# The last head group's output sums dealt anew over its slots, and weight maxima kept in columns, in a two-layer attention and spectral-filter kernel

## The chip, the core and the metric

One core of one Trainium2 chip. TensorE (PE) multiplies matrices and writes its sums to PSUM; VectorE (DVE), ScalarE (ACT) and GpSimd (POOL) work on elements; SyncE (SP) issues nearly all transfers. Each engine runs its own queue of instructions in order, and the engines wait for each other through semaphores. The metric is the device time of one launch in microseconds, median of the runs. All times in the text are microseconds (us) unless marked ns; times inside the profiled execution count from its first instruction.

## What is computed

Two attention blocks and two spectral filters in turn, each on a layer norm of its input and added to it, with S = 2048 rows, D = 1024 columns and 32 heads of 32:

```python
x = x + _A_ref(_layernorm(x), A_wqkv, A_wo)
x = x + _B_ref(_layernorm(x), B_w_r, B_w_i)
x = x + _A_ref(_layernorm(x), A_wqkv, A_wo)
x = x + _B_ref(_layernorm(x), B_w_r, B_w_i)
```

`_A_ref` projects to q, k and v, takes `softmax(q k^T / sqrt(32)) v` for each head and multiplies by `wo`. `_B_ref` is a real 2-D FFT over rows and columns, a product with complex weights `w_r + i w_i`, and the inverse FFT.

## The kernel before

One attention and one filter make a layer; the program runs two layers. Products of float32 data are made of float16 halves: a value is scaled and split into a high and a low part (`split`), and each product is three matmuls (high by high, high by low, low by high).

**Attention.** The heads go in 8 groups of 4 (`NG`). A group has 4 chunks of 512 query rows (`NCH`) by 16 tiles of 128 key rows (`NKT`), so 64 units. `S` (line 552) makes one unit's scores: 12 matmuls into two tiles of the pool `psS`, which has three tiles of two PSUM banks; the exponentials (line 562) read them on ScalarE into the pool `at_p` of eight buffers. `PV` (line 568) multiplies them by V, for two units at a time on every even unit; `add` (lines 579 and 581) keeps the running sums of the softmax on VectorE; `fin` (from line 583) turns these into factors at the end of a chunk, and `out` rounds the chunk's result to two halves. In the last group that result, `olast[c]`, stays in SBUF; it is made at the sixth unit of the following chunk.

Two units make a slot, 32 in a group. Behind an odd unit's scores the loop places other matmuls, which it draws from generators (`filler`, `wo_parts`): the projections of later groups, and in the last two groups the output product with `wo`. That product has 12 row tiles of 128 rows that are done here (the last four are done in the tail), each of 1024 columns in two halves. A half has 8 x 3 matmuls of 512 columns; those of the first seven head groups (21) can be made early. `wo_part` (line 456) makes these 21 into the one bank of the pool `psX`, and VectorE evacuates them with the residual added (line 466). `wo_rest` (line 496) makes the six that are left for a tile, three for each half, into a tile of `psS`; `wo_last` (line 470) evacuates it (line 475), takes the statistics of the next layer norm (line 477) and stores the rows (line 478); `mvs` holds the statistics of the 12 tiles. Four halves of 21 are placed in group 6. In group 7 each slot has either one half or one rest: the first rest stands in slot 11, and from there on a rest alternates with a half until all 20 halves and 12 rests are placed. In a slot with a rest, the six matmuls directly follow the odd unit's scores.

The order on PE and ACT in this part is the program's (`manual_schedule`). The order on VectorE, GpSimd and SyncE is made when the program is built, by a planner that takes the earliest ready instruction by its own estimate of times.

**The attention tail** (from line 679). The last four row tiles' output sums, the last chunk's `fin` and `out`, and the layer norm and first fold of all 16 row tiles for the filter, on VectorE for the larger part.

**The filter.** Its first loop (33 turns of `t1` and `fa`, lines 787 to 816) transposes on PE, multiplies, and splits the result on ACT (line 804) and VectorE (line 805). Its second loop goes over 32 units (`fb`, `fc`, `binv`, `cinv`): `loadw` (line 827) loads a unit's weights, GpSimd turns signs in them (line 846), and `fc` multiplies them in (lines 901 to 906: VectorE and GpSimd). A third loop transforms back.

**The flags.** While layer 0 runs, the kernel takes the largest magnitude of `wqkv` (lines 260 and 261, 48 pieces), `wo` (lines 784 and 785, 16 pieces, loaded for this in line 780 by `absmax`) and the filter weights (lines 837 and 838, 32 pieces): a reduction of a piece to one column, then a maximum with a running column. `combine_flags` (line 1124) decides from them at the end whether a general version must run instead; with these inputs it does not.

Of the kernel before, what the change touches and what calls it, by code (L numbers as in the profile page):

```python
# [226 lines left out]
class Weights:  # L227
# [5 lines left out]
    def prep(self, ph):  # L233
# [10 lines left out]
        st = []  # L244
# [11 lines left out]
        for i, (h, l, _) in enumerate(sl):  # L256
            split(nc, h, l, st[i], SW)
            if self.flag is not None:
                wm = ap.sm.tile([128, 1], F32, name="wm")
# [10 lines left out]
def attention(nc, tc, layer, ap, xin, yd, wts, wo, cst, dram, flags):  # L270
# [212 lines left out]
    def wo_parts():  # L483
        load_o(0)
        load_o(1)
        for t in [2, 3, 0, 1] + list(range(4, 12)):
# [7 lines left out]
    mvs = sm.tile([128, 24], F32, name="mvs")  # L494

# [112 lines left out]
    fill, lwo, wof = filler(), load_wo(), wo_parts()  # L608
    left, parts, rests = 16, 20, list(range(12))

# [14 lines left out]
    with tc.manual_schedule(engines={mybir.EngineType.PE, mybir.EngineType.Activation}):  # L625
        for g in range(NG):
# [3 lines left out]
            for u in range(NCH * NKT):  # L630
# [43 lines left out]
        run(wof)  # L674
        for t in rests:
            wo_rest(t)
    with tc.manual_schedule(engines={mybir.EngineType.PE}):
# [72 lines left out]
def spectral(nc, tc, ap, yd, xout, a, cst, fast, flags=None, nxt=None):  # L750
# [25 lines left out]
    def absmax(i):  # L776
# [5 lines left out]
        while len(wos) == 3 or (wos and i == 15):  # L782
            m = p3.tile([128, 1], F32, name="wom")
            nc.vector.tensor_reduce(m, wos.pop(0), axis=AX.X, op=ALU.max, apply_absolute_value=True)
            nc.vector.tensor_max(flags["w"], flags["w"], m)

# [40 lines left out]
    def loadw(i):  # L827
# [7 lines left out]
        if flags is not None:  # L835
            m = p2.tile([128, 1], F32, name="wbm")
            nc.vector.tensor_reduce(m, wt, axis=AX.X, op=ALU.max, apply_absolute_value=True)
            nc.vector.tensor_max(flags["wb"], flags["wb"], m)
        sa = fs.index(0) if g == 0 and 0 in fs else None
# [284 lines left out]
def combine_flags(nc, tc, pool, flags, cst):  # L1124

    f = pool.tile([128, 6], F32, name="f4")
    v = pool.tile([128, 1], F32, name="fv")
    nc.vector.tensor_reduce(v, flags["mv"][:, :, 1], axis=AX.X, op=ALU.min)
# [3 lines left out]
    nc.vector.tensor_scalar(f[:, 1:2], r, 1e20, None, op0=ALU.is_le)  # L1132
    nc.vector.tensor_scalar(f[:, 2:3], flags["w"], 1.0, None, op0=ALU.is_le)
    nc.vector.tensor_scalar(f[:, 3:4], flags["wb"], 2.0 ** -4, None, op0=ALU.is_le)
    nc.vector.tensor_scalar(f[:, 0:4], f[:, 0:4], -1.0, 1.0, op0=ALU.mult, op1=ALU.add)
    nc.vector.tensor_scalar(f[:, 4:5], flags["w"], 2.0 ** -7, None, op0=ALU.is_ge)
    nc.vector.tensor_scalar(f[:, 5:6], flags["wb"], 2.0 ** -12, None, op0=ALU.is_ge)
    with tc.tile_pool(name="flag_ps", bufs=1, space=PSUM) as ps:
# [18 lines left out]
def build(nc, tc, a):  # L1157
    with ExitStack() as ctx:
# [9 lines left out]
        for h in range(4):  # L1168
# [4 lines left out]
            "mv": cp.tile([128, 32, 2], F32, name="fmv"),  # L1173
            "w": cp.tile([128, 1], F32, name="fw"),
            "wb": cp.tile([128, 1], F32, name="fwb"),
# [3 lines left out]
        nc.vector.memset(flags["w"], 0.0)  # L1179
        nc.vector.memset(flags["wb"], 0.0)  # L1180
        nc.vector.memset(flags["r"], 0.0)
# [4 lines left out]
        for t in range(2):  # L1186
            nc.sync.dma_start(ap.x[:, t], x[t * 128:(t + 1) * 128, :])
        wts = [Weights(nc, ap, a["wp"], None if layer else flags["w"]) for layer in range(2)]
        for layer in range(2):
# [47 lines left out]
```

## Time and profile before

| What | us |
|---|---|
| Runs (three) | 3885.0, 3885.8, 3886.59; median 3885.8 |
| The profiled execution's own time | 3887.92 |
| Span from its first to its last instruction | 3886.0 |
| Granted TensorE clock, mean | 0.988 |
| Busy: TensorE, VectorE, ScalarE, GpSimd | 3738.1, 3181.9, 2901.1, 304.1 |
| Last head group, layer 0 (first scores to the tail's first matmul) | 1414.30 to 1647.25 |
| Attention tail, layer 0 | 1647.25 to 1705.26 |
| Filter, first loop and second loop, layer 0 | 1705.26 to 1755.1, to 1918.4 |
| Last head group and tail, layer 1 | 3340.5 to 3573.45, to 3621.3 |

A row of the profile names an engine, a line of the kernel, an operation, what it writes and reads (`out<-in`), and how often; a number in square brackets is the time for which the engine stood idle ahead of it, and what ended that wait. PEld is TensorE's loading of stationary operands, which overlaps its matmuls. A matmul's printed duration overlaps the next one's, so the pace is read from starts.

### The profile page before, as it was taken

How to read it: one execution, taken by the hardware profiler on the slowest of the kernel's cores; microseconds unless marked ns; L12 is line 12 of the kernel's file. 1: busy time of each engine (PE TensorE's matmuls, PEld its weight loads, DVE VectorE, ACT ScalarE, POOL GpSimd, SP SyncE). 2: the span in 40 equal slices, each digit the busy share in tenths (PEclk: the TensorE clock that was granted, in tenths of full speed). 3: DMA queues.
4: the chain of work that ended last, by engine and by line, in shares of the span. 5: the costliest groups of instructions: out<-in, count | busy, mean ns of one | idle time of the engine just before them, and what ended most of it. 6: DMA issues, size and time to landing. Idle time of an engine off the chain costs nothing.

```text
span 3886.0 us, 79635 instructions
## 1 busy us (share of the span) xinstructions
PE 3738.1 (96%) x32951; PEld 1644.2 (42%) x32951; DVE 3181.9 (82%) x3967; ACT 2901.1 (75%) x3567; POOL 304.1 (8%) x386
## 2 busy tenths in 40 slices
PE   6999999999999999989989999999999999999998
PEld 4322433343234233368854334333433432333788
DVE  6689899989998987966675998989899889788544
ACT  4578887888788865657855888888888888666686
POOL 1000000000000000014320000000000000000143
PEclk9999999999999999999999999999999999999999
DMA  8000000000000221134270000000000002111333
GB/s 204 15 12 23 12 12 17 18 12 18 12 26 7 73 70 64 62 142 140 62 179 12 15 23 12 12 18 18 12 20 12 23 12 90 53 69 66 147 99 105
DMA packets 165575, 194.08 MB, mean 50 GB/s; under 512 B 74961, under 2 KB 120657, under 8 KB 164177
## 3 DMA queue, kind: packets, MB, share of 16 engines
q1 hardware_dynamic: 164912, 188.82, 15.6%
q8 instruction: 260, 4.26, 0.5%
q14 instruction: 115, 0.93, 0.1%
q10 hardware_dynamic: 288, 0.07, 0.0%
HBM read 123.83 MB, written 48.23 MB: 44 GB/s over the span
## 4 chain that ended last, share of the span: by engine, by line
PE 73%; DVE 12%; issue 7%; ACT 3%; DMA 3%; POOL 1%; SPq 0%; DVEq 0%; ACTq 0%; POOLq 0%
PE o L568 20%; PE s L558 17%; PE x L340 12%; PE x L384 7%; PE x L443 6%; DVE R L581 3%; ACT p L562 2%; PE ps L862 2%; PE ps L800 2%; PE s L587 1%; PE ps L791 1%; DMA w<-in_w 1%; PE s L443 1%; PE o L384 1%; PE ps L977 1%
## 5 line engine op out<-in xcount | busy, mean ns | idle before, releaser
L562 ACT ACTIVATE p<-s,bias 128x1024 f32<-128x1024 f32 x2048 | 2169.7, 1112 | 575.4 <-PE s L558 564.5
L581 DVE TENSOR_TENSOR R<-R,p 128x1024 f32<-128x1024 f32 x1792 | 2089.0, 1218 | 139.4 <-ACT p L562 136.3
L568 PE MATMUL o<-p,R 128*32 128x512 f32 x8192 | 985.5, 599 | 0.0
L340 PE MATMUL x<-big,wqk 128*128 128x512 f16 x2880 | 684.2, 383 | 17.0 <-DVE Q L168 6.3
L558 PEld LDWEIGHTS <-R 32*128 32x128 f16 x12288 | 233.0, 92 | 769.3 <-issue 654.3
L340 PEld LDWEIGHTS <-wqk 128*128 128x128 f16 x3072 | 277.3, 98 | 452.9 <-issue 159.1
L558 PE MATMUL s<-Q,R 32*128 32x512 f16 x6144 | 433.0, 378 | 12.0 <-ACT p L562 10.7
L558 PE MATMUL s<-R 32*128 32x512 f16 x6144 | 432.3, 379 | 8.2 <-ACT p L562 6.7
L568 PEld LDWEIGHTS o<-p,R 128*32 128x32 f32 x8192 | 213.8, 109 | 524.6 <-issue 524.0
L384 PEld LDWEIGHTS <-big 128*128 128x128 f16 x3072 | 296.5, 100 | 155.5 <-issue 73.9
L384 PE MATMUL x<-wv,big 128*128 128x256 f16 x2688 | 324.1, 277 | 34.5 <-DMA big<-hl 34.5
L579 DVE SCALAR_TENSOR_TENSOR R<-p 128x1024 f32<-128x1024 f32 x128 | 153.9, 1203 | 196.1 <-ACT p L562 195.7
L443 PE MATMUL x<-big 128*128 128x512 f16 x1050 | 237.4, 380 | 0.0
L365 POOL PARTITION_ALL_REDUCE mall<-mqk x16 | 40.7, 2542 | 2333.8 <-DVE mqk L359 2322.5
L443 PEld LDWEIGHTS <-big 128*128 128x128 f16 x1344 | 126.2, 98 | 178.0 <-issue 34.6
L910 DVE TENSOR_TENSOR H<-G,H 128x512 f16<-128x512 f32 (+1 forms) x68 | 46.5, 683 | 105.4 <-ACT H L909 105.3
L862 PE MATMUL ps<-cbi,H 128*128 128x256 f16 (+1 forms) x792 | 99.2, 273 | 6.0 <-ACT H L909 3.7
L855 ACT COPY U<-ps 64x256 f32<-64x256 f32 (+1 forms) x272 | 97.2, 357 | 8.4 <-PE ps L862 3.3
L855 ACT COPY B<-ps 64x256 f32<-64x256 f32 (+1 forms) x272 | 97.1, 357 | 6.7 <-PE ps L862 2.4
L862 PE MATMUL ps<-cb,big 128*128 128x256 f16 x780 | 96.3, 273 | 0.0
L805 DVE TENSOR_TENSOR big<-ps,big 128x512 f16<-128x512 f32 x64 | 44.5, 695 | 58.5 <-ACT big L804 58.5
L167 ACT ACTIVATE R<-x 128x512 f16<-128x512 f32 x88 | 52.7, 598 | 50.5 <-PE x L340 50.4
(429 smaller groups left out, 2992.5 us busy)
## 6 DMA issues: line engine op xcount, KB each, us to landing
wst<-in_wp SPq DMA_DIRECT2D x96, 256.0 KB, 3.0
R<-y SPq DMA_DIRECT2D x32, 512.0 KB, 5.4
w<-in_w SPq DMA_DIRECT2D x60, 256.0 KB, 2.7
od<-ohl SPq DMA_DIRECT2D x56, 256.0 KB, 2.4
big<-od SPq DMA_DIRECT2D x16, 896.0 KB, 6.7
y<-R SPq DMA_DIRECT2D x20, 512.0 KB, 2.7
R<-in_x SPq DMA_DIRECT2D x16, 512.0 KB, 5.8
wst<-in_wo SPq DMA_DIRECT2D x32, 256.0 KB, 3.0
```

The costliest lines, as they stand in the source:

```text
L167: nc.scalar.activation(hi, src, AF.Copy, scale=scale)
L340: nc.tensor.matmul(ps, a, b, start=d == 0 and i == 0, stop=d == 7 and i == 2)
L384: nc.tensor.matmul(ps[:, j], l, r, start=d == 0 and i == 0, stop=d == 7 and i == 2)
L443: nc.tensor.matmul(p, a, b, start=start and d == ds[0] and i == 0, stop=stop and d == ds[-1] and i == 2)
L558: nc.tensor.matmul(s[h // 2][:, h % 2], K[g][r, a, kt * 128:kt * 128 + 128], Q[g][r, b, c * 512:c * 512 + 512], start=i == 0, stop=i == 2)
L562: nc.scalar.activation(p, s[hf], AF.Exp, bias=bias[g], scale=SCALE / (SQ * SQ))
L568: nc.tensor.matmul(O[g, c][32 * h:32 * h + 32], V[g][:, kt, 32 * h:32 * h + 32], P[g, c, kt, h // 2][:, h % 2], start=kt == 0, stop=kt == ...
L579: nc.vector.scalar_tensor_tensor(acc[hf], P[g, c, 0, hf], 1e-34, p, op0=ALU.add, op1=ALU.add)
L581: nc.vector.tensor_add(acc[hf], acc[hf], p)
L800: nc.tensor.matmul(pa[:, j], tt[:, j], mm[:, g], start=True, stop=True)
L855: nc.scalar.copy(ov[64 * r:64 * r + 64, a0:a0 + m, x], tl[64 * x:64 * x + 64, :m, r])
L862: nc.tensor.matmul(out, l, r, start=k == 0, stop=k == len(mm_) - 1)
```

## The change

In the last group the 426 matmul steps of the halves are given out by a list, `share`, one number for each of the 32 slots, and the rests stand in slots 11, 12, 14, 15, 20, 22, 24, 26, 28, 29 and 30, in a slot behind its other matmuls. The first ten slots keep a whole half of 21 steps; slots 10 to 15 get 7 each, slots 16 to 27 get 11 and 10 in turn, and the last four get 12. Tile 11 has no rest: its halves are made of all 24 matmuls, and its statistics and store follow there.

Each maximum of a weight piece goes to a column of its own (64 columns for `wqkv` and `wo`, 32 for the filter weights), so the running maxima and the two memsets fall away, and `combine_flags` reduces the columns first. The reductions of `wo`'s pieces are tied to their place in the program: each comes on VectorE directly behind the split that was traced before it, in the filter's first loop.

```diff
-                nc.vector.tensor_reduce(wm, st[i], axis=AX.XY, op=ALU.max, apply_absolute_value=True)
-                nc.vector.tensor_max(self.flag, self.flag, wm)
+                nc.vector.tensor_reduce(self.flag.pop(), st[i], axis=AX.XY, op=ALU.max, apply_absolute_value=True)
...
-    def wo_part(c, t, dst):
+    def wo_part(c, t, dst, nd):
 
         x = xres(c, t)
+        st = sm.tile([128, 2, 6], F32, name="st")
         for n in range(2):
             p = bank()
-            m = wo_mm(p, c, t, n, range(7))
-            for _ in range(20):
+            m = wo_mm(p, c, t, n, range(nd))
+            for _ in range(3 * nd - 1):
                 next(m)
                 yield
             run(m)
             sl = slice(n * 512, n * 512 + 512)
             nc.vector.scalar_tensor_tensor(dst[:, sl], p, 1.0 / (SO * SW), x[:, sl], op0=ALU.mult, op1=ALU.add)
+            if nd == 8:
+                nc.vector.bn_stats(st[:, n], dst[:, sl])
+                if n:
+                    r0 = c * 512 + t * 128
+                    nc.sync.dma_start(yd[r0:r0 + 128, :], dst)
+                    nc.vector.bn_aggr(mvs[:, 8 * c + 2 * t:8 * c + 2 * t + 2], st)
             yield
...
-            yield from wo_part(t // 4, t % 4, wo_dst[t])
+            yield from wo_part(t // 4, t % 4, wo_dst[t], 8 if t == 11 else 7)
...
-    left, parts, rests = 16, 20, list(range(12))
+    left, rests = 16, {}
+    share = [21] * 10 + [7] * 6 + [11, 10] * 6 + [12] * 4
+    for t, n in zip(range(11), (11, 12, 14, 15, 20, 22, 24, 26, 28, 29, 30)):
+        rests[n] = t
...
-                    t = rests[0] if rests else 16
-                    if (t // 4 < c - 1 or t // 4 == c - 1 and kt >= 7) and (kt % 4 == 3 or not parts):
-                        wo_rest(rests.pop(0))
-                    elif parts:
-                        parts -= 1
-                        for _ in range(21):
-                            next(wof)
+                    for _ in range(share[u // 2]):
+                        next(wof)
+                    if u // 2 in rests:
+                        wo_rest(rests[u // 2])
...
-            m = p3.tile([128, 1], F32, name="wom")
-            nc.vector.tensor_reduce(m, wos.pop(0), axis=AX.X, op=ALU.max, apply_absolute_value=True)
-            nc.vector.tensor_max(flags["w"], flags["w"], m)
+            tc.keep_in_program_order(nc.vector.tensor_reduce(flags["wcol"].pop(), wos.pop(0), axis=AX.X, op=ALU.max, apply_absolute_value=True))
...
-            m = p2.tile([128, 1], F32, name="wbm")
-            nc.vector.tensor_reduce(m, wt, axis=AX.X, op=ALU.max, apply_absolute_value=True)
-            nc.vector.tensor_max(flags["wb"], flags["wb"], m)
+            nc.vector.tensor_reduce(flags["wb"][:, i:i + 1], wt, axis=AX.X, op=ALU.max, apply_absolute_value=True)
...
+    fw, fb = (pool.tile([128, 1], F32, name=n) for n in ("fwm", "fwbm"))
+    nc.vector.reduce_max(fw, flags["w"], axis=AX.X)
+    nc.vector.reduce_max(fb, flags["wb"], axis=AX.X)
```

More of the change, by code (lines that the diff above doesn't have):

```diff
@@ L453, in xres @@
         return x
-    def wo_part(c, t, dst):
+    mvs = sm.tile([128, 24], F32, name="mvs")
+    def wo_part(c, t, dst, nd):
         x = xres(c, t)
+        st = sm.tile([128, 2, 6], F32, name="st")
         for n in range(2):
             p = bank()
-            m = wo_mm(p, c, t, n, range(7))
-            for _ in range(20):
+            m = wo_mm(p, c, t, n, range(nd))
+            for _ in range(3 * nd - 1):
                 next(m)
@@ L485, in wo_parts @@
         load_o(1)
-        for t in [2, 3, 0, 1] + list(range(4, 12)):
+        for t in (2, 3, 0, 1, 4, 5, 6, 7, 8, 9, 10, 11):
             if t == 8:
@@ L489, in wo_parts @@
                 wo_dst[8], wo_dst[9] = two[:, 0], two[:, 1]
-            yield from wo_part(t // 4, t % 4, wo_dst[t])
+            yield from wo_part(t // 4, t % 4, wo_dst[t], 8 if t == 11 else 7)
             if t in (1, 7):
                 load_o(t // 4 + 2)
-    mvs = sm.tile([128, 24], F32, name="mvs")
     def wo_rest(t):
@@ L674, in attention @@
         run(wof)
-        for t in rests:
-            wo_rest(t)
     with tc.manual_schedule(engines={mybir.EngineType.PE}):
@@ L1124, in combine_flags @@
 def combine_flags(nc, tc, pool, flags, cst):
+    assert not flags["wcol"]
     f = pool.tile([128, 6], F32, name="f4")
+    fw, fb = (pool.tile([128, 1], F32, name=n) for n in ("fwm", "fwbm"))
+    nc.vector.reduce_max(fw, flags["w"], axis=AX.X)
+    nc.vector.reduce_max(fb, flags["wb"], axis=AX.X)
     v = pool.tile([128, 1], F32, name="fv")
@@ L1173, in build @@
             "mv": cp.tile([128, 32, 2], F32, name="fmv"),
-            "w": cp.tile([128, 1], F32, name="fw"),
-            "wb": cp.tile([128, 1], F32, name="fwb"),
+            "w": cp.tile([128, 64], F32, name="fw"),
+            "wb": cp.tile([128, 32], F32, name="fwb"),
             "r": cp.tile([128, 16], F32, name="fr"),
@@ L1178, in build @@
         }
-        nc.vector.memset(flags["w"], 0.0)
-        nc.vector.memset(flags["wb"], 0.0)
+        flags["wcol"] = [flags["w"][:, i:i + 1] for i in range(64)]
         nc.vector.memset(flags["r"], 0.0)
@@ L1187, in build @@
             nc.sync.dma_start(ap.x[:, t], x[t * 128:(t + 1) * 128, :])
-        wts = [Weights(nc, ap, a["wp"], None if layer else flags["w"]) for layer in range(2)]
+        wts = [Weights(nc, ap, a["wp"], None if layer else flags["wcol"]) for layer in range(2)]
         for layer in range(2):
```

9 lines of the change are left out of this document (4 added, 5 removed).

## The prediction, made before the changed kernel was run

> **What bounds the kernel now.** I read the page first, then the busy time by stage, then the single instructions of the stages that the change touches. The page says that TensorE (PE) does the work and that VectorE (DVE) is close behind.
>
> ```profile
> PE 3738.1 (96%) x32951; PEld 1644.2 (42%) x32951; DVE 3181.9 (82%) x3967; ACT 2901.1 (75%) x3567; POOL 304.1 (8%) x386
> ```
>
> An average over stages says nothing about one edit, so the next view is a table by stage: the last head group of layer 0 in two stretches (slots 0 to 9 and the start of slot 10; then slots 10 to 31), the attention tail of layer 0 and that of layer 1, the filter's first loop with two pieces of it, and the filter's second loop in layer 0 and in layer 1. Columns: stretch, length, busy time and count of PE, PEld, DVE, ACT, POOL; then PE clock, DMA share, GB/s.
>
> ```profile
> core 0 of [0], span 3886.0 us
> core 0: us, PE busy (x) PEld busy (x) DVE busy (x) ACT busy (x) POOL busy (x), PEclk, DMA share, GB/s
> 1414.30:1499.76 85.46, 85.46 (x667) 29.52 (x667) 57.62 (x62) 45.98 (x45) 0.00 (x0) 1.00 0.18 62
> 1499.76:1647.25 147.49, 142.15 (x1159) 45.77 (x1155) 132.27 (x148) 93.79 (x91) 0.00 (x0) 1.00 0.18 67
> 1647.25:1705.26 58.01, 42.88 (x205) 18.76 (x201) 49.28 (x105) 20.14 (x21) 11.62 (x33) 0.90 0.48 161
> 3573.45:3621.30 47.85, 42.72 (x205) 18.77 (x201) 39.43 (x74) 20.03 (x21) 11.64 (x33) 0.98 0.27 95
> 1705.26:1755.10 49.84, 49.84 (x384) 49.58 (x385) 21.18 (x33) 37.16 (x63) 0.00 (x0) 0.94 0.27 108
> 1715.00:1720.00 5.00, 5.00 (x43) 5.00 (x43) 2.58 (x4) 4.04 (x8) 0.00 (x0) 1.00 0.56 230
> 1720.00:1725.00 5.00, 5.00 (x42) 5.00 (x42) 2.26 (x4) 3.83 (x8) 0.00 (x0) 1.00 0.01 3
> 1755.10:1918.40 163.30, 153.08 (x1302) 135.92 (x1300) 104.46 (x256) 132.42 (x340) 70.49 (x102) 1.00 0.32 104
> 3670.60:3822.40 151.80, 147.60 (x1303) 134.27 (x1301) 73.97 (x190) 130.52 (x340) 70.65 (x102) 1.00 0.36 113
> ```
>
> Three things are to be seen. PE is never idle in the first stretch of the last head group, and is short of work by 5.3 us in the second. The two tails do the same matmuls (x205 each), yet layer 0's takes 10.16 us longer, with 9.85 us more on VectorE. The filter's first loop is PE from end to end, with VectorE busy for 21.18 of 49.84 us; its second loop is 11.5 us longer in layer 0 than in layer 1.
>
> **Part 1, the deal of the output sums.** One slot with a rest, PE's instructions in order:
>
> ```profile
> 1504.40 0.83 PE L558 MATMUL s<-Q,R 32*128 32x512 f16 x12
> 1505.16 1.92 PE L568 MATMUL o<-p,R 128*32 128x512 f32 x16
> 1507.01 0.82 PE L558 MATMUL s<-Q,R 32*128 32x512 f16 x12
> 1507.77 1.47 PE L443 MATMUL s<-big,ohl 128*128 128x512 f16 x6
> 1509.17 0.39 PE L558 MATMUL s<-Q,R 32*128 32x512 f16 x2
> 1510.05 0.82 PE L558 MATMUL s<-Q,R 32*128 32x512 f16 x10 [0.48 <-ACT p L562]
> 1510.80 1.92 PE L568 MATMUL o<-p,R 128*32 128x512 f32 x16
> 1512.65 0.40 PE L558 MATMUL s<-Q,R 32*128 32x512 f16 x4
> ```
>
> An unhindered block of scores takes 1505.16 - 1504.40 = 0.76 us. The block behind the rest takes from 1509.17 to 1510.80 = 1.63 us: after two matmuls it stands until ScalarE (ACT) has finished an exponential and freed a score buffer, because the rest itself has taken one of the three. The rest covers only 1509.17 - 1507.77 = 1.40 us of the two exponentials' wait. Each such slot loses 0.87 us. How many do, in this group:
>
> ```profile
> its engine sat idle before it (us, times) until:
>   ACT p L562: 5.3, 11
> ```
>
> Eleven (the twelfth rest has no scores behind it), so 11 x 0.87 = 9.6 us a layer. Layer 1 has the same structure, hence 19.1 us in all.
>
> After the change the rest always stands behind 7 to 12 other matmuls of the same slot, each 1.40/6 = 0.23 us, so 1.6 us or more is added to the 1.40, against 1.40 + 0.87 = 2.27 needed. The wait for the exponential is gone from all eleven. The matmuls themselves are the same: before 12 x (42 + 6) = 576 a layer, after 11 x 48 + 48 = 576. Slots 0 to 9 keep their 21 matmuls, so the first stretch stays as it is. The second becomes 147.49 - 9.6 = 137.9 us at best.
>
> What is late next is VectorE. It has the same work in that stretch, 132.27 us, so it goes from 90% to 96%. The wait to look at is the score buffer that a rest holds until its evacuation (L475) is done:
>
> ```profile
> 1509.02 1.23 DVE L581 TENSOR_TENSOR R<-R,p 128x1024 f32<-128x1024 f32 x1 [0.25 <-ACT p L562]
> 1510.16 1.22 DVE L475 SCALAR_TENSOR_TENSOR R<-s,R 128x1024 f32<-128x1024 f32 x1
> ```
>
> The rest ends at 1509.17; one running sum (L581) is ahead, and the evacuation ends at 1511.38. The scores that need that buffer stood at 1512.65, and without the lost 0.87 would stand at 1511.78: 0.40 us of slack. With a second running sum ahead (1510.16 - 1509.02 = 1.14 us) PE waits 0.74. The trace cannot show how often that happens in the new order, so I bound it: never (0), and at every one of the 22 rests (16.3 us). I take one rest in four, 22/4 x 0.74 = 4.1 us, since the scores at 1512.65 start without a wait for it, and VectorE has 4% left.
>
> Tile 11 is now summed whole (24 matmuls a half, through the other bank), with its two statistics and its aggregate on VectorE: the same instructions as its rest had, apart from two evacuations of 512 columns where there were two of 512 and one of 1024, about one running sum less. Its store and those of the other eleven stay at twelve, later or earlier in SyncE's queue by a slot or so; what reads them back comes only in the second loop. The residual loads go out one per tile as before. I cost these at nothing: the stretch's DMA share is 0.18, and the cover is the slack of a slot; without it a late residual load would hold one half's evacuation, at most 3 us once.
>
> **Part 2, wo's maxima.** Now the planner has put them into the attention tail of layer 0, where VectorE sets the pace:
>
> ```profile
> 1679.53 0.69 DVE L784 TENSOR_REDUCE wom<-wo 128x1 f32<-128x512 f32 x1 [1.78 <-DMA wo<-in_wo]
> 1680.13 1.22 DVE L475 SCALAR_TENSOR_TENSOR xres<-s,xres 128x1024 f32<-128x1024 f32 x1
> ```
>
> ```profile
> 1681.40 0.81 PE L443 MATMUL s<-big 128*128 128x512 f16 x3 [1.80 <-DVE xres L475]
> ```
>
> The reduction waits for its DMA, the evacuation stands behind it, and PE waits 1.80 us for the evacuation. Sixteen of 0.69 are 11.0 us of VectorE. Taken away, the tail should look like layer 1's, which is the same work without them: 58.01 - 47.85 = 10.2 us gained. Bounds: 0 (they are only moved, below) and 11.0 plus the sixteen running maxima.
>
> In the first loop the sixteen need 11.0 us of the 49.84 - 21.18 = 28.7 us that VectorE has free there, and the split (L805) behind each is late by 0.69 at most, with eight PSUM banks between it and PE. Their loads move too: three go out early as before, thirteen from inside the loop, each when a buffer is freed three reductions earlier, that is six turns of 49.84/33 = 1.5 us, 9 us ahead of use. On SyncE's queue they come behind the constants; the DMA engines are still at 0.56 in 1715 to 1720 and idle after. The first moved load goes out about seven turns after 1705.26, at 1716, and is wanted at turn 11, at 1722. So nothing is lost, with 0 to 5 us as bounds.
>
> A rule of the Trainium skill speaks against fixing them in place: "TensorE: Matmul & The Clock Gate", in the table that opens the page, gives VectorE a queue of 8 in strict first-in first-out order, so a reduction whose load is late holds everything behind it. The quoted pair (0.69 behind 1.78 of DMA wait, evacuation behind both) agrees. What it would do here is the third rival.
>
> **Part 3, maxima in own columns.** 96 running maxima and two memsets go; two short reductions come at the end and can be placed anywhere after the maxima. The 48 of wqkv and the two reductions lie beside a busy PE; I cost them at nothing, at 1 us if a few in the prologue are not covered. The 32 of the filter's weights, in the second loop:
>
> ```profile
> 1868.64 0.69 DVE L837 TENSOR_REDUCE wbm<-w 128x1 f32<-128x512 f32 x1
> 1869.24 0.41 DVE L902 TENSOR_TENSOR t__20499<-ps,w 128x256 f32<-128x256 f32 x1
> 1869.57 0.57 DVE L838 TENSOR_TENSOR fwb<-fwb,wbm 128x1 f32<-128x1 f32 x1
> ```
>
> ```profile
> 1869.40 0.73 POOL L846 TENSOR_TENSOR w<-w,sg 128x256 f32<-128x256 f32 x1 [2.59 <-DVE wbm L837]
> 1870.09 0.73 POOL L905 TENSOR_TENSOR G<-G,t__20499 128x256 f32<-128x256 f32 x1
> 1870.89 0.72 POOL L906 TENSOR_TENSOR G<-G,t__20499 128x256 f32<-128x256 f32 x1
> ```
>
> Here GpSimd's three run back to back, so the maximum (L838) is off the path: it delays products that GpSimd could not take sooner. It is on the path only where GpSimd waits:
>
> ```profile
> POOL G L905 <- DVE t__20435 L902: 0.5, 1, 0.5
> POOL G L905 <- DVE t__20160 L902: 0.5, 1, 0.5
> POOL G L905 <- DVE t__20306 L902: 0.5, 1, 0.5
> ```
>
> Three or four times 0.5: I take 2.0 us. The bounds are 0 and 11.5 us, layer 0's whole excess over layer 1; the reduction L837, which stays, carries most of that.
>
> The skill's page "SBUF — State Buffer", section "SBUF: two separate sides", says that a VectorE instruction with two SBUF inputs and a GpSimd instruction exclude each other for a whole instruction. The 0.57 us of a one-column maximum beside L846 agrees. By the rule alone each such maximum would give back its blocked time; by GpSimd's rows little of it reaches the path, and I keep 2.0.
>
> **The sum.** -19.1 + 4.1 - 10.2 - 2.0 = -27.2 us. The profiled execution took 3887.92 us (span 3886.0), which is 2.1 over the median of the three runs, 3885.8; taken off both, 3860.7 and 3858.6 us.
>
> **The rivals.** *VectorE becomes the bound of the last group:* every rest waits 0.74, 16.3 us, and the sum is -19.1 + 16.3 - 10.2 - 2.0 = -15.0, so 3871 us. For it: 96%; against: rests in before get their evacuation after one running sum.
> *Slower:* the planner puts four running sums ahead of each evacuation instead of one. The score buffer comes back 3 x 1.14 - 0.40 = 3.0 us late, 22 times, 66 us; with the other gains 3885.8 - 31.3 + 66 = 3921 us. It decides from 31.3/22 = 1.42 us of wait per rest, so about 1.6 running sums more than now. Against it: four are a slot's whole supply, and they would all have to be ready first.
> *wo's maxima are only moved:* each holds L805 and the loop grows by what the tail loses; -17.0, so 3869 us. For it: the fixed order; against: 28.7 us free.
> *The second loop falls to layer 1's pace* because the planner orders VectorE anew without the maxima: 9.5 us more, 3849 us. Against it: L837 stays.
>
> **Chances.** The forecast 0.69 (its own range 3850 to 3866), VectorE-bound 0.13, only moved 0.05, layer 1's pace 0.07, slower 0.06. The range 3847 to 3873 holds all but the slower case and the edges. A change under 0.2% (7.8 us) cannot be told from none here: faster 0.92, same 0.02, slower 0.06.
>
> **What would show it.** Waits of scores (L558) for ACT p in the last group near 0 instead of 11; the second stretch near 140 us; PE's wait for L475 small; layer 0's tail near 48 us with no L784 in it; the first loop at 50 us with sixteen L784 inside; the second loop near 161. Wrong would be: L558 waiting for DVE at most rests, or L805 late behind L784.

## The result, and the profile after

The changed kernel takes 3855.85 us (median of four runs, 3852.02 to 3858.89) against 3885.4 (four runs, 3882.65 to 3886.59): the ratio is 0.992, with a 95% interval of 0.9908 to 0.9932. The forecast was 3858.6, with a range of 3847 to 3873. The profiled execution took 3855.25 us, 32.7 less than that of before.

The page's line of busy times, changed kernel:

```profile
PE 3720.5 (97%) x32951; PEld 1640.1 (43%) x32951; DVE 3165.8 (82%) x3869; ACT 2898.3 (75%) x3567; POOL 303.0 (8%) x386
```

The matmuls are the same in number (x32951); VectorE has 98 instructions fewer. The same table by stage as before the change: the last head group of layer 0 in two stretches, the tails of layer 0 and layer 1, the filter's first loop, its second loop in layer 0 and in layer 1.

```profile
core 0 of [0], span 3853.3 us
core 0: us, PE busy (x) PEld busy (x) DVE busy (x) ACT busy (x) POOL busy (x), PEclk, DMA share, GB/s
1403.04:1488.50 85.46, 85.46 (x667) 29.52 (x666) 57.63 (x62) 45.92 (x45) 0.00 (x0) 1.00 0.19 62
1488.50:1629.44 140.94, 138.16 (x1159) 44.99 (x1155) 135.32 (x150) 93.50 (x91) 0.00 (x0) 1.00 0.20 74
1629.44:1677.28 47.84, 42.71 (x204) 18.79 (x200) 35.75 (x68) 19.99 (x21) 11.60 (x33) 0.98 0.32 110
3540.99:3588.84 47.85, 42.71 (x204) 18.78 (x200) 36.15 (x71) 19.99 (x21) 11.59 (x33) 0.98 0.25 86
1677.28:1726.81 49.53, 49.53 (x385) 49.26 (x385) 28.83 (x46) 37.08 (x63) 0.00 (x0) 0.95 0.48 175
1726.81:1889.73 162.92, 153.11 (x1302) 136.65 (x1300) 94.79 (x231) 131.99 (x340) 70.30 (x102) 0.98 0.34 106
3638.33:3789.59 151.26, 147.21 (x1303) 134.28 (x1300) 74.52 (x190) 130.25 (x340) 70.12 (x102) 1.00 0.35 113
```

Read against the table of before, stretch for stretch: the last group's first part is as it was (85.46), the second is 6.55 us shorter (147.49 to 140.94), layer 0's tail is 10.17 shorter and now equals layer 1's, the first loop has taken in thirteen of the sixteen reductions (VectorE 21.18 to 28.83) and is no longer than before, and the second loop is 0.4 shorter with 9.7 us less on VectorE.

**The last group.** Its waits on TensorE, in full (what waited, what for; us in total, times, longest):

```profile
PE s L563 <- DVE R L482: 2.8, 3, 1.4
```

The line numbers have moved by a few: L563 is the scores (L558 before), L482 the evacuation of a rest (L475). The eleven waits for an exponential are gone; three waits for an evacuation stand in their place. The longest of them, in the order of time, on TensorE and then on VectorE:

```profile
1522.47 1.92 PE L573 MATMUL o<-p,R 128*32 128x512 f32 x16
1525.83 0.83 PE L563 MATMUL s<-Q,R 32*128 32x512 f16 x12 [1.44 <-DVE R L482]
```

```profile
1519.47 3.44 DVE L586 TENSOR_TENSOR R<-R,p 128x1024 f32<-128x1024 f32 x3
1522.83 0.68 DVE L467 SCALAR_TENSOR_TENSOR R<-x,xres 128x512 f32<-128x512 f32 x1
1523.43 1.22 DVE L586 TENSOR_TENSOR R<-R,p 128x1024 f32<-128x1024 f32 x1
1524.56 1.22 DVE L482 SCALAR_TENSOR_TENSOR R<-s,R 128x1024 f32<-128x1024 f32 x1
```

The rest was done at about 1521.7. VectorE finishes a running sum, then takes the evacuation of a half (L467) and another running sum (L586), and only then the rest's; the score buffer comes back at 1525.78. Over both layers, none to two running sums come between a rest and its evacuation.

**The start of the second loop.** On VectorE, the first loop's last split, wo's last reduction and the second loop's first one; then TensorE's wait; then two of SyncE's own waits (L835 is the load of filter weights, L783 the load of a piece of wo):

```profile
1728.42 0.68 DVE L806 TENSOR_TENSOR big<-ps,big 128x512 f16<-128x512 f32 x1
1729.90 0.69 DVE L786 TENSOR_REDUCE fw<-wo 128x1 f32<-128x512 f32 x1 [0.80 <-DMA wo<-in_wo]
...
1734.47 0.69 DVE L837 TENSOR_REDUCE fwb<-w 128x1 f32<-128x512 f32 x1 [3.38 <-DMA w<-in_w]
```

```profile
1739.12 0.61 PE L861 MATMUL ps<-cbi,H 128*128 128x256 f16 x2 [4.22 <-ACT H L908]
```

```profile
SPq L783 <- DVE fw L786: 22.8, 9, 4.2
...
SPq L835 <- DVE fw L786: 3.7, 1, 3.7
```

The sixteenth reduction ends at 1730.59, after the last split, and the load of the first filter weights waits for it, because these weights take over the first loop's memory (its pools are closed there, and new ones opened). The two rows of before that answer to the last two:

```profile
1760.36 0.69 DVE L837 TENSOR_REDUCE wbm<-w 128x1 f32<-128x512 f32 x1 [3.74 <-DMA w<-in_w]
```

```profile
1765.09 0.39 PE L862 MATMUL ps<-cbi,H 128*128 128x256 f16 x2 [1.56 <-ACT H L909]
```

The first weights land 7.66 us after the second loop's first matmul (1734.47 less 1726.81), before the change 5.25 us (1760.36 less 1755.11). TensorE waits 4.22 us where it waited 1.56, and the two matmuls behind the wait take 0.61 instead of 0.39: the granted clock is 0.50 from 1737.10 to 1743.80. The first loop hides the reductions, but not the tail of the chain of loads.

**Where the time went, by stage.** Each length runs from the first matmul of a stage to that of the next; the last group is counted here to its last product with V.

| Stage | before | changed | difference | forecast |
|---|---|---|---|---|
| Groups 0 to 5, layer 0 | 1107.3 | 1097.7 | -9.6 | 0 |
| Last group, both layers | 2 x 232.42 | 2 x 225.87 | -13.1 | -15.0 |
| Tail, layer 0 | 58.54 | 48.38 | -10.2 | -10.2 |
| Second loop, layer 0 | 163.32 | 162.92 | -0.4 | -2.0 |
| Group 6, layer 1 | 182.47 | 184.99 | +2.5 | 0 |
| All the rest | | | -1.9 | 0 |

Two rows were not in the forecast, and the fourth was the sum of two larger things. The experiments are about these.

### The profile page after: what moved, and what is told of

Its sections match the earlier page's. It is cut to its first block, busy times and chain, and to the rows that moved or that the text cites. A ratio compares the mean times of both kernels' runs of the same rounds, so it can differ in the third digit from the quotient of the medians.

```text
span 3853.3 us, 79584 instructions
## 1 busy us (share of the span) xinstructions
PE 3720.5 (97%) x32951; PEld 1640.1 (43%) x32951; DVE 3165.8 (82%) x3869; ACT 2898.3 (75%) x3567; POOL 303.0 (8%) x386
## 4 chain that ended last, share of the span: by engine, by line
PE 73%; DVE 12%; issue 8%; ACT 3%; DMA 2%; POOL 2%; SPq 0%; DVEq 0%; POOLq 0%; ACTq 0%
PE o L573 19%; PE s L563 16%; PE x L338 12%; PE x L382 7%; PE x L441 6%; DVE R L586 4%; PE s L441 2%; PE ps L861 2%; PE ps L801 2%; ACT p L567 1%; PE s L592 1%; PE ps L792 1%; DMA wst<-in_wp 1%; PE ps L976 1%; PE ps L930 1%
## 5 line engine op out<-in xcount | busy, mean ns | idle before, releaser
L586 DVE TENSOR_TENSOR R<-R,p 128x1024 f32<-128x1024 f32 x1792 | 2085.4, 1219 | 111.2 <-ACT p L567 107.8
L563 PEld LDWEIGHTS <-R 32*128 32x128 f16 x12288 | 231.6, 92 | 760.3 <-issue 644.6
L563 PE MATMUL s<-R 32*128 32x512 f16 x6144 | 430.9, 378 | 10.6 <-ACT p L567 8.9
L563 PE MATMUL s<-Q,R 32*128 32x512 f16 x6144 | 425.4, 378 | 7.5 <-DVE R L482 5.5
```

What stands on the lines that cost most here:

```text
L563: nc.tensor.matmul(s[h // 2][:, h % 2], K[g][r, a, kt * 128:kt * 128 + 128], Q[g][r, b, c * 512:c * 512 + 512], start=i == 0, stop=i == 2)
L586: nc.vector.tensor_add(acc[hf], acc[hf], p)
```

## The experiments

The theory after this comparison: deal and tail do what the forecast says, the filter weights' columns gain about 5 us, and the chain of wo's loads takes as much away at the start of the second loop. Rivals: the second loop's gain is small, as forecast, and its start has another cause; and the gain in groups 0 to 5 is chance of the clock and not the change's.

Each ran beside the kernel before on the same chip; the ratios are to it. The deal and the maxima come first, then the parts of the maxima with what they led to; wqkv's stand near the end. They ran in three batches, and the median of the kernel before was another in each: 3885.55 us beside the deal alone, all the maxima, wo's alone and wqkv's alone; 3886.5 beside the filter weights' alone, wo's maxima earlier, the rests ahead and the rests spread; 3889.46 beside the others. Between batches the ratios are the better comparison.

**The deal alone.** The new shares, the rests' places and tile 11, with all maxima as before.

```diff
-    left, parts, rests = 16, 20, list(range(12))
+    left, rests = 16, {}
+    share = [21] * 10 + [7] * 6 + [11, 10] * 6 + [12] * 4
...
```

> Only the new deal of the output sums in the last group; all maxima as before. My theory: the eleven waits of the scores for an exponential go in both layers and a few waits for a rest's evacuation (3 a layer, 2.8 us in the changed kernel) come, so the last group is 6.6 us shorter in each layer, 225.9 instead of 232.4, and the run about 13 us shorter (3872). The attention tail of layer 0 stays at 58.5 and groups 0 to 5 of layer 0 stay as before, within what the granted clock does from run to run (each half-clock stretch costs about 1.5 us). Rival: the last group gains only because VectorE has no running maxima elsewhere or because of a new order that the whole change brings; then it stays near 232.

Measured: 3870.79 us, ratio 0.9956 (0.9943 to 0.997), 14.8 us less. The last group of layer 0 and its tail:

```profile
1413.60:1639.44 225.84, 223.08 (x1819) 74.43 (x1820) 192.36 (x211) 139.59 (x136) 0.00 (x0) 1.00 0.20 69
1639.45:1695.52 56.07, 43.24 (x209) 18.77 (x201) 46.76 (x102) 20.10 (x21) 11.93 (x33) 0.93 0.50 165
```

The group's gain is the deal's own, to 0.03 us. The tail is 2.5 us shorter though nothing in it was changed: VectorE's order in it is another, and the granted clock is 0.93 where it was 0.90. Which of the two does it is not shown.

**All the maxima, the old deal.**

```diff
-                nc.vector.tensor_max(self.flag, self.flag, wm)
...
-            nc.vector.tensor_max(flags["w"], flags["w"], m)
...
-            nc.vector.tensor_max(flags["wb"], flags["wb"], m)
...
```

> Only the maxima: own columns for all three weights and wo's reductions tied to the first loop; the deal as before. My theory: the tail of layer 0 falls from 58.5 to 48.4 us, both last groups stay at 232.4, the second loop loses 0.5 to 2. Groups 0 to 5 of layer 0 were 10.5 us shorter in the changed kernel: theory A, the 48 running maxima of wqkv were ahead of splits for which PE waits, and without them it falls below the length at which the clock is halved; then these groups are about 10 us shorter here too and the run is 21 us shorter, 3864. Theory B, the halved clock comes by chance of phase; then these groups are anywhere between 0 and 10 us shorter, and the run 11 to 21 us shorter.

Measured: 3869.37 us, ratio 0.9955 (0.9942 to 0.9969), 16.2 less. Tail 48.38, last groups 232.42 and 232.43, second loop 162.71, groups 0 to 5 of layer 0 1099.1. The halves of the change add up: 14.8 + 16.2 = 31.0 us against 29.5 for the whole.

**wo's maxima alone, tied.**

```diff
-            m = p3.tile([128, 1], F32, name="wom")
-            nc.vector.tensor_reduce(m, wos.pop(0), axis=AX.X, op=ALU.max, apply_absolute_value=True)
-            nc.vector.tensor_max(flags["w"], flags["w"], m)
+            tc.keep_in_program_order(nc.vector.tensor_reduce(flags["wcol"].pop(), wos.pop(0), axis=AX.X, op=ALU.max, apply_absolute_value=True))
...
```

> Only wo's maxima: columns of their own and tied to the first loop; wqkv, the filter's weights and the deal as before. My theory: the tail of layer 0 falls from 58.5 to 48.4 us, the first loop stays at 49.5 to 50 with sixteen reductions in it, nothing else changes by more than the clock's chance: 10 us less, 3875. Rival: the reductions hold the splits of the first loop, which grows by up to 10 us; then the run is unchanged.

Measured: 3882.75 us, ratio 0.9991 (0.9982 to 1.0001), 2.8 less, which is not clear of none. The tail and the second loop:

```profile
1649.04:1697.41 48.37, 43.24 (x208) 18.77 (x200) 39.55 (x72) 20.02 (x21) 11.64 (x33) 0.99 0.35 121
1747.41:1915.90 168.49, 155.35 (x1302) 137.21 (x1300) 106.53 (x263) 132.32 (x340) 70.52 (x102) 0.98 0.33 103
```

The tail gives its 10.2 us, and the first loop stays at 50.00, as the theory had it. But the second loop is 5.2 us longer than before, which neither theory had: half of the gain is lost a stage later. This pointed to the start of the second loop, and so to the next pair.

**The filter weights' maxima alone.**

```diff
-            m = p2.tile([128, 1], F32, name="wbm")
-            nc.vector.tensor_reduce(m, wt, axis=AX.X, op=ALU.max, apply_absolute_value=True)
-            nc.vector.tensor_max(flags["wb"], flags["wb"], m)
+            nc.vector.tensor_reduce(flags["wb"][:, i:i + 1], wt, axis=AX.X, op=ALU.max, apply_absolute_value=True)
...
```

> Only the filter weights' 32 running maxima go; wo's and wqkv's maxima and the deal as before. Theory A: the second loop of layer 0 falls from 163.3 to about 157.5 us, because the changed kernel's 162.9 is the sum of this gain, some 5.5, and of a loss at its start (the first weights of the second loop land 2.4 us later behind wo's last loads, and the clock is halved after a wait of 4.2 us); the run is 5 to 6 us shorter than before, 3880. Theory B (my prediction's sum): 2.0 us at most, the second loop near 161.5. Rival: nothing, 163, and the loop of 168.5 in the kernel with wo's maxima alone has another cause.

Measured: 3880.12 us, ratio 0.9985 (0.9976 to 0.9994).

```profile
1752.94:1913.95 161.01, 153.51 (x1303) 136.56 (x1300) 93.08 (x225) 132.29 (x340) 70.55 (x102) 0.99 0.33 105
```

The loop is 2.3 us shorter, which is theory B's number; the timed run is 6.4 us shorter (interval 2.3 to 9.3), which is theory A's. The trace decides: after a wait of 1.63 us at the loop's start this profile has a stretch at half clock (0.50 from 1763.90 to 1767.20), where the kernel before, after 1.56 us, has none. So the loop is cut in two. Its last two thirds, from the same product on, in the kernel before, in this one and in the changed kernel:

```profile
1811.00:1918.43 107.43, 100.64 (x845) 88.61 (x844) 68.24 (x163) 89.25 (x233) 46.36 (x68) 1.00 0.17 49
```

```profile
1811.00:1913.95 102.95, 98.90 (x845) 88.32 (x844) 59.48 (x143) 89.01 (x233) 46.20 (x68) 1.00 0.18 51
```

```profile
1787.10:1889.73 102.63, 98.84 (x845) 88.31 (x844) 59.27 (x144) 88.95 (x233) 46.23 (x68) 1.00 0.18 51
```

4.5 and 4.8 us less for the same 845 matmuls, while the first third is 2.2 us longer here than before (58.06 against 55.89). ScalarE's waits for GpSimd's last product in these last two thirds, before and changed:

```profile
ACT H L909 <- POOL G L906: 14.7, 20, 1.1
```

```profile
ACT H L908 <- POOL G L905: 10.0, 17, 1.1
```

4.7 us less, and 4.5 less with the filter weights' columns alone (10.2 in 17 waits). So the running maxima cost more than twice what I took. That they did it by delaying the chain from VectorE's products through GpSimd to ScalarE is what these waits suggest; the planner also orders VectorE anew without them, and no run parts the two.

**wo's maxima earlier.** The changed kernel, with the sixteen reductions in every turn from turn 10 to 23, done well ahead of the loop's end.

```diff
-        if i % 2:
-            absmax(i // 2)
+        absmax(i - 8)
```

> The changed kernel with wo's maxima in each turn of the first loop from turn 10 to 23 instead of in every second turn up to the end. Theory A (the last loads of wo hold up the second loop's first weights): the second loop of layer 0 starts with a PE wait of about 1.6 us instead of 4.2 and without a half-clock stretch, and is 157 to 158 us long instead of 162.9; the run 5 us shorter than the changed kernel, 3851. Rival: the reductions, now in each turn (0.68 of 1.48 us beside a split of 0.69), hold the splits and the first loop grows by 2 us or more. Rival: the start's wait has another cause; the second loop stays at 162.9.

Measured: 3853.76 us, ratio 0.9916 (0.9902 to 0.993). First and second loop, and TensorE's wait at the second loop's start:

```profile
1687.81:1737.49 49.68, 49.68 (x385) 49.41 (x386) 30.91 (x52) 37.13 (x63) 0.00 (x0) 0.95 0.50 180
1737.49:1895.88 158.39, 151.62 (x1302) 135.60 (x1300) 93.72 (x225) 132.34 (x340) 70.20 (x102) 1.00 0.34 107
```

```profile
1747.31 0.39 PE L860 MATMUL ps<-cbi,H 128*128 128x256 f16 x2 [1.41 <-ACT H L907]
```

Theory A holds: the wait is 1.41 us, the clock does not fall, and the second loop is 158.4, 4.5 us less, while the first loop is 0.15 longer. So in the changed kernel's 162.92, 4.5 us were the late weights and the clock behind them; without these the second loop would have gained 4.9. By the medians the whole run shows only 2.1 of the 4.5, within its scatter (3849.61 to 3862.44).

**wo's maxima not tied.** The changed kernel without the tie; own columns kept.

```diff
-            tc.keep_in_program_order(nc.vector.tensor_reduce(flags["wcol"].pop(), ...
+            nc.vector.tensor_reduce(flags["wcol"].pop(), ...
```

> The changed kernel without the tie of wo's maxima to their place in the program; own columns as in the changed kernel. Theory A: the tie alone takes them out of the attention tail; without it the planner puts them back there, the tail of layer 0 is 58 us and the second loop starts without its wait of 4.2 us and is 158 to 159 us long: 5 to 6 us longer than the changed kernel in sum, 3861. Rival: without the chain through the running maximum the planner leaves them out of the tail by itself, and the kernel is like the changed one, 3856, or better.

Measured: 3858.77 us, ratio 0.992 (0.9903 to 0.9936). Tail and second loop:

```profile
1635.29:1690.55 55.26, 43.24 (x208) 18.77 (x201) 45.65 (x87) 20.09 (x21) 11.55 (x33) 0.91 0.50 167
1739.65:1898.51 158.86, 151.58 (x1302) 135.58 (x1300) 93.14 (x225) 132.30 (x340) 70.73 (x102) 1.00 0.34 107
```

The planner puts all sixteen back into the tail, which is 6.9 us longer than the changed kernel's; the second loop is 4.1 shorter. The tie is what empties the tail, and it gives back more than half of that. The 2.8 us that are left do not show in the timed runs: the ratio is the changed kernel's, 0.992.

**The rests ahead of the other matmuls.** The changed kernel, same slots and shares, the two statements in the other order.

```diff
+                    if u // 2 in rests:
+                        wo_rest(rests[u // 2])
                     for _ in range(share[u // 2]):
                         next(wof)
-                    if u // 2 in rests:
-                        wo_rest(rests[u // 2])
```

> The changed kernel with each rest ahead of the other matmuls of its slot instead of behind them: the same shares and the same slots. My theory (the rest takes one of three score buffers, and what stands behind it must cover two exponentials): the 7 to 12 matmuls behind the rest cover the exponential as well as ahead of it, since both stand between the odd unit's scores and the next, so no wait for an exponential comes back; but the evacuation has 1.6 us or more longer, so the waits for it (three a layer, 2.8 us) shrink. The last group is then 223 to 226 us. Rival: the rest has to wait for its own buffer, which an exponential still holds, and loses 0.5 to 0.9 us in most of the eleven slots: the last group is 229 to 233.

Measured: 3856.22 us, ratio 0.9926 (0.9909 to 0.9943).

```profile
1405.30:1631.23 225.93, 223.97 (x1821) 74.41 (x1820) 192.10 (x211) 139.48 (x136) 0.00 (x0) 1.00 0.20 70
```

225.93 against 225.87: no difference, though the waits are others. The waits for an evacuation shrank from 2.8 us to 0.6, as the theory had it, and a rest waited once for its own buffer, for 0.2; but a wait of 1.1 us for a running sum came, and TensorE is busy for 0.9 us longer with the same matmuls (223.97 against 223.09), which stays unexplained. That the other matmuls stand in the same slot as the rest is what covers the exponential; on which side of it they stand does not matter.

**The rests spread, first try.** Rests in slots 11, 13, 15 and 17, the shares made even around them.

```diff
-    share = [21] * 10 + [7] * 6 + [11, 10] * 6 + [12] * 4
-    for t, n in zip(range(11), (11, 12, 14, 15, 20, 22, 24, 26, 28, 29, 30)):
+    share = [21] * 10 + [8, 7] + [9, 7] * 3 + [11, 10] * 5 + [12] * 4
+    for t, n in zip(range(11), (11, 13, 15, 17, 20, 22, 24, 26, 28, 29, 30)):
```

> The changed kernel with its rests in slots 11, 13, 15 and 17 instead of 11, 12, 14 and 15, and the 63 matmuls of slots 10 to 17 dealt as 8, 7, 9, 7, 9, 7, 9, 7. My theory (the three waits for a rest's evacuation, 0.93, 0.39 and 1.44 us, come where short slots with rests follow one another and VectorE is behind): they shrink to one or none, and the last group is 223 to 224.5 us in each layer instead of 225.9; the run is 3 to 5 us shorter. Rival: VectorE is behind by its whole work in these slots (the running sums of both units and the evacuation), wherever the rest stands; then the waits only move, and the group stays near 225.9.

Measured: 3862.72 us, ratio 0.9944 (0.993 to 0.9958): slower than the changed kernel, against the theory, though the two intervals just overlap (0.993 to 0.9932). The last group is 229.11 us. TensorE's waits in it:

```profile
PE x L441 <- DVE R L467: 4.0, 2, 2.6
PE s L563 <- DVE R L482: 0.2, 1, 0.2
```

The waits for a rest's evacuation did shrink, from 2.8 to 0.2. But two halves now end in the middle of a slot, and the next half, which needs the same single bank of `psX`, stands behind its evacuation (L467) with nothing between. The changed kernel's shares 7, 7, 7 and 11, 10 sum to 21: each half ends with its slot, and scores and products with V cover the evacuation. That property was in the list of numbers, and I had not seen it.

**Both, with the shares left alone.** Rests in slots 11, 13, 15 and 17, the changed kernel's shares, and the earlier maxima of wo.

```diff
-    for t, n in zip(range(11), (11, 12, 14, 15, 20, 22, 24, 26, 28, 29, 30)):
+    for t, n in zip(range(11), (11, 13, 15, 17, 20, 22, 24, 26, 28, 29, 30)):
...
-        if i % 2:
-            absmax(i // 2)
+        absmax(i - 8)
```

> The changed kernel with wo's maxima in each turn of the first loop from turn 10 to 23, and with its rests in slots 11, 13, 15 and 17 instead of 11, 12, 14 and 15, the shares left as they are, so that every half still ends with its slot. Theory A: e8_spread lost 3 us a layer because two halves ended in the middle of a slot and the next half had to wait for the one bank (4.0 us); with the shares left alone this wait is gone, and the waits for a rest's evacuation are fewer than the three of the changed kernel: the last group 223 to 225 us in each layer, the second loop of layer 0 158.4, the run 6 to 8 us under the changed kernel, 3848 to 3850. Rival: VectorE is behind in these slots by its whole work; the last group stays at 225.9 or above, and the run is 4 to 5 us under the changed kernel, 3851.

Measured: 3849.08 us (four runs, 3846.45 to 3852.84), ratio 0.9898 (0.9881 to 0.9915). The last group and the second loop of layer 0, and the waits in the group:

```profile
1406.23:1630.72 224.49, 223.02 (x1821) 74.39 (x1820) 191.91 (x211) 139.59 (x136) 0.00 (x0) 1.00 0.20 69
1728.77:1887.18 158.41, 151.46 (x1302) 135.59 (x1300) 92.89 (x225) 132.39 (x340) 70.65 (x102) 1.00 0.34 108
```

```profile
PE s L563 <- DVE R L482: 1.5, 2, 1.0
```

1.4 us less in each last group and 4.5 in the second loop make 7.3 us by stages; the median is 6.8 under the changed kernel's, and by the two ratios the difference is some 8.5. The two intervals against the kernel before overlap slightly (0.9908 to 0.9915).

**wqkv's maxima alone.** This and the two repeats that follow ask for the 9.6 us in groups 0 to 5.

```diff
-                nc.vector.tensor_reduce(wm, st[i], axis=AX.XY, op=ALU.max, apply_absolute_value=True)
-                nc.vector.tensor_max(self.flag, self.flag, wm)
+                nc.vector.tensor_reduce(self.flag.pop(), st[i], axis=AX.XY, op=ALU.max, apply_absolute_value=True)
...
```

> Only wqkv's 48 running maxima go, each piece's maximum has its own column; all else as before. Theory A (running maxima delay the splits that PE waits for): groups 0 to 5 of layer 0 are about 10 us shorter and no half-clock stretch is in them after 140 us, the run about 11 us shorter, 3874. Theory B (chance of phase): half-clock stretches in these groups are found here too, three or four of them, each 1.5 us; then the groups are 2 to 5 us shorter at most, from waits of 0.3 to 0.5 us less at each place.

Measured: 3882.17 us, ratio 0.9989 (0.998 to 0.9998), 3.4 less; groups 0 to 5 are 1102.6 us, 4.7 less than in the first profile of before. That is theory B's size, with two half-clock stretches after 140 us where A had none and B three or four. The four parts alone (14.8, 2.8, 6.4 and 3.4) add up to 27.4 us against 29.5 for the whole.

**The kernel before and the changed kernel, once more, unaltered.**

> The kernel before, once more. Theory B (which waits of PE are followed by a half clock is chance): groups 0 to 5 of layer 0 differ from the first profile's 1107.3 us by 2 us or more, with other places at half clock, while last groups, tails and groups 1 to 5 of layer 1 agree to 0.1 us. Rival: these groups repeat to 0.5 us, and the 10.5 us by which they were shorter in the changed kernel are the change's own.

> The changed kernel, once more. Theory B: groups 0 to 5 of layer 0 are 2 us or more longer than the first profile's 1097.7, with half-clock stretches in them, of which the first profile had none after 140 us; group 6 of layer 1 is not 185.0 again but anywhere from 182 to 185.5. Rival: both repeat to 0.5 us.

Groups 0 to 5 of layer 0 in one view each: before, before again, changed, changed again.

```profile
125.21:1232.52 1107.31, 1085.29 (x10201) 384.21 (x10201) 996.86 (x1078) 892.39 (x948) 23.53 (x24) 0.99 0.05 16
```

```profile
124.32:1236.96 1112.64, 1089.03 (x10201) 384.74 (x10201) 996.71 (x1078) 891.70 (x948) 22.36 (x24) 0.99 0.05 16
```

```profile
123.59:1221.26 1097.67, 1077.13 (x10201) 382.10 (x10202) 991.47 (x1041) 891.64 (x948) 26.21 (x24) 1.00 0.05 16
```

```profile
126.39:1227.03 1100.64, 1081.22 (x10201) 383.02 (x10201) 991.62 (x1041) 892.26 (x948) 26.25 (x24) 0.99 0.05 16
```

The same program differs by 5.3 and by 3.0 us here, while groups 1 to 5 of layer 1 agree to 0.3 us in all fourteen profiles. So theory B holds, and theory A in part: over all profiles of this study the five with running maxima of wqkv have 1106.0 to 1112.6 (mean 1108.8), and the nine without have 1097.7 to 1105.5 (mean 1100.8). By the traces' record of the granted clock, the five have 3 to 7 half-clock stretches in these groups after 140 us (mean 4.8), the nine have none to 4 (mean 2.0). So about 8 us in the mean goes with the change; the first pair's 9.6 held some luck. What remains open is why the timed gain of wqkv's columns alone (3.4, interval 0.8 to 7.8 us) lies at half of it; in that kernel's profile, group 6 of layer 1 takes 1.6 of its 4.7 us back (184.09 against 182.47).

Group 6 of layer 1 was 184.99 in the first profile of the changed kernel and 182.81 in the second, so the +2.5 does not come in every execution. Whether the change makes it likelier is open: it takes 184.0 us or more in five of the nine profiles without wqkv's running maxima, and 182.1 to 182.5 in all five with them. In the first profile of the changed kernel, ScalarE's split of a piece of wo came late, and the scores behind it:

```profile
3252.96 0.63 ACT L167 ACTIVATE big<-wst 128x512 f16<-128x512 f32 x1 [4.68 <-DMA wst<-in_wo]
```

## Why the prediction was right, and where it was right by luck

The forecast was 27.2 us, the medians differ by 29.5; the terms fit less well than their sum.

*The exponentials' wait* (-19.1): right. Eleven waits became none in both layers, and the deal alone gives the same group to 0.03 us. A group is 6.55 us shorter with 2.8 of new waits in it, so about 9.35 came back where 9.6 were forecast.

*The new wait for the evacuation* (+4.1, one rest in four at 0.74): right in kind and about in size. Three of eleven rests a layer wait, 2.8 us, so 5.6 in all. Each costs 0.93 on average and not 0.74, because the evacuation of a half can stand ahead too, which I had not counted. That VectorE would be at 96% in the second stretch was met, but from other figures: 135.32 of 140.94 us where I had 132.27 of 137.9. Some 3 us of its work came into the stretch from the tail (layer 1's tail: 39.43 before, 36.15 after, with the same matmuls). This did not make it the bound.

*wo's maxima out of the tail* (-10.2): met to 0.05 us. Layer 1's tail, the same work without them, was the right price tag.

*"So nothing is lost"* in the first loop: wrong, though the loop itself did not grow. I followed each load to its own reduction, found it 9 us ahead of use, and stopped there. Three of the sixteen reductions came behind the loop's last matmul. The last of the chain was not followed to what comes behind it on SyncE: the first weights of the second loop wait for the sixteenth reduction. 4.5 us, inside the 0 to 5 that I had named as the bound for it, but for another reason.

*The filter weights' running maxima* (-2.0): mis-sized; 4.8 to 4.9. I read three GpSimd waits of 0.5 us as all of the path. The wait that shrank with the loop was ScalarE's, for GpSimd's last product, 14.7 us in twenty waits, and I had left it out. A one-column maximum took 0.15 us at the shortest and 0.57 in the median of the loop's 32, like the one beside GpSimd's product in the prediction's rows. VectorE had 20 of them in the last two thirds of the loop, where its busy time fell by 8.97 us (68.24 to 59.27), of which 4.8 reached the end. The Trainium skill ("SBUF — State Buffer", section "SBUF: two separate sides") says that a VectorE instruction with two SBUF inputs and a GpSimd instruction that reads SBUF shut each other out for the whole instruction; the 0.57 against 0.15 agrees, and I gave the rule too little.

These last two errors nearly cancel, and that is luck: 4.9 gained and 4.5 lost make -0.4, against -2.0.

*wqkv's maxima at nothing, "1 us if a few in the prologue are not covered"*: wrong. They do not lie beside a busy TensorE everywhere: it waits for single splits on VectorE in each group, and each such wait can cost a stretch at half clock besides. About 8 us by the means of the profiles, 3.4 by the timed run. This gain was not in the sum. Without it the change would be worth 21.5 to 26.1 us, less than the forecast; that the total came so near is luck in part.

The rivals: VectorE as the bound did not come; three rests of eleven waited, not all. The slower case is refuted: none to two running sums came ahead of an evacuation, not four. The reductions did not hold the splits of the first loop (49.53 us).

## What to carry to other kernels

Where loads are moved to the end of a stage, follow the last of them to the first load of the next stage: it shares the queue and the memory. Work that shares a single bank should be dealt so that its evacuation falls where other matmuls stand; a list of step counts can hide that. A small instruction is priced by the waits of all the engines behind it, and not by whether the next one is busy: VectorE was busy for only 64% of the loop's last two thirds (68.24 of 107.43 us), and the small maxima still cost 4.8 us.

## What the hardware showed that I had not expected

A short wait of TensorE can be followed by a stretch at half clock. Twelve matmuls of the first head group, before the change and after it:

```profile
245.61 4.25 PE L340 MATMUL x<-big,wqk 128*128 128x512 f16 x12 [2.15 <-DVE Q L168]
```

```profile
242.59 2.75 PE L338 MATMUL x<-big,wqk 128*128 128x512 f16 x12 [2.48 <-DVE Q L168]
```

After a wait of 2.15 us they take 4.25 us, after one of 2.48 only 2.75. Their stretches, before and changed, with the mean granted clock at 0.63 and 1.00:

```profile
245.61:249.79 4.18, 4.18 (x13) 1.38 (x13) 4.18 (x5) 0.01 (x1) 0.00 (x0) 0.63 0.01 4
```

```profile
242.59:245.28 2.69, 2.69 (x14) 1.08 (x14) 2.69 (x4) 0.00 (x0) 0.00 (x0) 1.00 0.02 6
```

Within the first, the clock is 0.50 from 246.70 on. This fall costs about 1.5 us on top of the wait itself. Before the change four waits of 1.90 to 2.24 us in groups 0 to 5 were followed by one; in the changed kernel's first profile none was, in its second two. The Trainium skill ("TensorE: Matmul & The Clock Gate", section "Part 1: The HAM clock gate") has the clock fall after an idle window of about 3.4 us, and the window running free of the program. The chance from run to run agrees with the second; the waits here were shorter than the first. That shorter waits bring fewer falls is what the counts for groups 0 to 5 suggest (4.8 and 2.0 in the mean); no experiment here varied a wait by itself.
